# A fused attention, channel-mixing and expert kernel: the split channel weights are kept in DRAM and loaded as two parts

## The chip, the cores and the metric

The kernel runs on one core of a Trainium2 chip. Its engines each run their own instruction stream, in order: PE (matrix products, with PEld loading the stationary operand), DVE and ACT (element-wise work), POOL (element-wise work and indirect DMAs) and SP, which here issues all plain DMAs. An instruction that waits for a semaphore holds up everything behind it on its engine. The metric is device time in microseconds of one execution; a profile of one such execution gives the rows that are read below.

## The reference, cut to what matters

The program computes three blocks in a row for 4 batches of 576 tokens: attention in which scores more than `tau` below the row's maximum are dropped, a channel block, and a block of 8 experts of which each token takes one.

```
attn = softmax(where(scores >= max(scores) - tau, scores, -1e9)) @ v
u  = x + (x.T @ U @ V).T
y  = u + relu(u @ w_ch1) @ w_ch2          # 512 -> 2048 -> 512
e  = expert of the token (arg-max of logits, or the token before's)
out[b, s] = p[e] * (relu(y[b, s] @ w1[e]) @ w2[e])
```

All data are float32. The change is about `w_ch1` and `w_ch2`, the channel weights.

## The kernel before

**Split operands.** A product of the channel block is made of three faster ones: each operand is split into a high part of type F32R (ACT writes a copy of the float32 tile in that type) and a low part (the tile less its high part). The products are high by high, high by low and low by high, summed in PSUM. `w0h` and `w0l` are the parts of a chunk of `w_ch1`, `w1h` and `w1l` those of `w_ch2`; `uh`, `ul` those of the activations, `hh`, `hl` those of the hidden layer.

**Stages.** Attention of batch 0 runs first, alone. Then three mixed stages follow: the channel block of batch b-1 is interleaved with the attention of batch b (the costs 82 and 65 given to `interleave` set the mix). The channel block of batch 3 then runs beside the first steps of the experts (`early_slots`), and at last the experts run alone. The channel block goes over 16 chunks f of the hidden width: `mlp_l1(b, f)` (24 products, lines 610 to 612) for each chunk, and after the chunks 4, 8, 12 and at the end `mlp_l2` over four chunks (96 products, lines 627 to 629).

**How a chunk comes in.** The weights arrive as 64-bit floats. `convert` turns them into float32 once, in 512-column pieces (`cr` loads on line 180, ACT and DVE steps, stores to the DRAM tensor `wdram` on line 219), during the attention of batch 0 and the first mixed stage. `load_w(b, f)` (line 583) then serves every batch: for each of the two halves it loads a float32 tile `wr` of 256 KB from `wdram` (line 592), lets ACT write the high part (line 595) and POOL the low part (line 596). It is called two chunks ahead, at the end of chunk f for chunk f+2. `wr` has 6 buffers, `w0h`/`w0l` have 2 each and `w1h`/`w1l` 5 each. With 2 buffers the parts of chunk f+2 can be written only when `mlp_l1` of chunk f has read its own; with 5 buffers the `w1` parts of chunks 5 to 8 wait for the first `mlp_l2`, and so on.

**What sets the order.** The program is written in one order, and a scheduler with its own costs places each engine's instructions; only during the attention of batch 0 is POOL, and in the experts SP, held to the written order. SP's list thus mixes the weight loads with the attention's loads (`raw`, `v`), the conversion's loads and stores, the stores of finished rows (`ydram`, line 677) and the expert weights (`ew`, line 959).

**The experts' start.** The rows of the first expert are fetched by POOL with indirect DMAs into `yg` tiles (line 1023), which take buffers of the tag `wr`; PE turns them (`y0p`, `y1p`, `y2p`, line 1032), each into the same PSUM tile after ACT and DVE have emptied it (lines 1034, 1035).

Of the kernel before, what the change touches and what calls it, by code (L numbers as in the profile page):

```python
# [8 lines left out]
F32 = mybir.dt.float32  # L9
# [5 lines left out]
AF = mybir.ActivationFunctionType  # L15
ALU = mybir.AluOpType
# [6 lines left out]
FF = 2048  # L23
# [32 lines left out]
WR = 6  # L56
# [27 lines left out]
def attention_channel_moe(ctx, tc, qk, vv, tau, umat, vrep, wch, wgl, wexp, consts, out):  # L84
    nc = tc.nc
    pe, dve, act, pool, sp = nc.tensor, nc.vector, nc.scalar, nc.gpsimd, nc.sync

    cp = ctx.enter_context(tc.tile_pool(name="cp", bufs=1))
    dr = ctx.enter_context(tc.tile_pool(name="dr", bufs=1, space=DRAM))
    ydram = dr.tile([NTOK, DM], F32, name="ydram")  # L90
    wdram = dr.tile([FF, 1024], F32, name="wdram")

    cst = cp.tile([128, C_W], F32, name="cst")
    ident = cst[:, C_ID:C_ID + 128]
# [19 lines left out]
    mlp = p1.enter_context(tc.tile_pool(name="mlp", bufs=1))  # L114
# [468 lines left out]
    def load_w(b, f):  # L583
        nm = f"{b}_{f}"
        if f >= NF or nm in W:
            return
        while DONE[0] < f:
            next(conv, None)
        r = []
        for i, bufs in ((0, W0), (1, W1)):  # L590
            x = mlp.tile([128, 512], F32, tag="wr", name=f"wr{nm}_{i}", bufs=WR)
            sp.dma_start(out=x, in_=wdram[f * 128:f * 128 + 128, i * 512:i * 512 + 512])
            hi = mlp.tile([128, 512], F32R, tag=f"w{i}h", name=f"w{i}h{nm}", bufs=bufs)
            lo = mlp.tile([128, 512], F32R, tag=f"w{i}l", name=f"w{i}l{nm}", bufs=bufs)
            act.activation(hi, x, AF.Copy)  # L595
            pool.tensor_tensor(out=lo, in0=x, in1=hi.bitcast(F32), op=ALU.subtract)  # L596
            r.append((hi, lo))
        W[nm] = r

# [33 lines left out]
    def channel(b):  # L633
        hs = {}
        load_w(b, 0)
        load_w(b, 1)
        for f in range(NF):
            yield from mlp_l1(b, f, hs)
            if f % 4 == 0 and f:
                yield from mlp_l2(b, f - 4, hs)  # L640
            load_w(b, f + 2)
        HS[b] = hs
# [373 lines left out]
    rows, yts = {}, {}  # L1016
# [228 lines left out]
```

## Time and profile before

| | us |
|---|---|
| median of 3 runs | 1111.4 (1111.2 to 1113.02) |
| the profiled execution | 1110.32 |
| its span in the profile | 1108.5 |
| PE busy in the span | 1037.1 (94%) |
| attention alone / mixed stages / last channel block / experts (ends read from PE's rows) | 123 / 123 to 686 / 686 to 812 / 812 to the end |

The span is the profiled execution less what lies around it (1.8 us). A row of a table of stretches gives each engine's busy time in the stretch with its number of instructions, the granted clock of TensorE as a share of full speed, the mean busy share of the 16 DMA engines, and GB/s. Idle time of PE is what a change to its feeders can give back; idle time of another engine matters only where PE waits for it.

### The profile page before, as it was taken

The numbers are of one execution on the slowest core, as the hardware profiler recorded it, in microseconds if no ns is written. First come the engines' busy times: TensorE is split into PE (matmuls) and PEld (weight loads), VectorE is DVE, ScalarE is ACT, GpSimd is POOL, SyncE is SP. The second block draws the span as 40 slices with busy tenths as digits, with TensorE's granted clock in tenths as the row PEclk, the third lists the DMA queues.
The fourth block names the chain that finished last, engine by engine and source line by source line (L and its number), as shares of the span: only waits on it lengthen the run. The fifth ranks groups of instructions, "written<-read, shape, count | busy, mean of one in ns | idle before, by whom it ended". The sixth has DMA issues, their size and how long they took to land. (4 is left out here: it accounts for less than half of the span.)

```text
span 1108.5 us, 19450 instructions
## 1 busy us (share of the span) xinstructions
PE 1037.1 (94%) x7170; PEld 910.7 (82%) x7170; DVE 687.5 (62%) x1617; ACT 581.6 (52%) x1220; POOL 313.4 (28%) x246
## 2 busy tenths in 40 slices
PE   6788899999999999999999999999999999999995
PEld 4566788889888889988898998979878788889874
DVE  6898776776465666646656554552458664456573
ACT  5788676674554556546464554332333344445462
POOL 1221123142222314221241222234411433233231
PEclk9899999999999999999999999989999999999998
DMA  6544577762223124132321211352243465456550
GB/s 199 184 152 138 181 247 227 240 214 93 88 92 95 58 78 126 53 99 77 94 70 42 67 49 55 114 213 82 77 138 133 129 222 162 153 175 200 186 170 15
DMA packets 57992, 143.83 MB, mean 130 GB/s; under 512 B 7133, under 2 KB 7901, under 8 KB 57888
## 3 DMA queue, kind: packets, MB, share of 16 engines
q1 hardware_dynamic: 54528, 132.27, 37.4%
q0 software_dynamic: 3360, 10.23, 2.8%
q8 instruction: 58, 0.95, 0.4%
q14 instruction: 46, 0.38, 0.1%
HBM read 124.65 MB, written 18.61 MB: 129 GB/s over the span
## 5 line engine op out<-in xcount | busy, mean ns | idle before, releaser
L610 PE MATMUL l<-uh,w0h 128*128 128x256 f32 (+1 forms) x512 | 157.9, 308 | 4.5 <-DVE hl L614 2.1
L596 POOL TENSOR_TENSOR w1l<-wr,w1h 128x512 fp32r<-128x512 f32 x64 | 81.7, 1299 | 269.7 <-ACT w1h L595 246.2
L627 PE MATMUL l<-hh,w1h 128*128 128x256 f32 (+1 forms) x512 | 157.4, 307 | 0.2 <-DVE yT L630 0.2
L612 PE MATMUL l<-uh,w0l 128*128 128x256 f32 (+1 forms) x512 | 153.7, 300 | 2.8 <-POOL w0l L596 2.8
L596 POOL TENSOR_TENSOR w0l<-wr,w0h 128x512 fp32r<-128x512 f32 x64 | 85.0, 1327 | 243.4 <-ACT w0h L595 233.8
L611 PE MATMUL l<-ul,w0h 128*128 128x256 f32 (+1 forms) x512 | 153.3, 299 | 0.0
L628 PE MATMUL l<-hl,w1h 128*128 128x256 f32 (+1 forms) x512 | 152.8, 298 | 0.0
L629 PE MATMUL l<-hh,w1l 128*128 128x256 f32 (+1 forms) x512 | 152.2, 297 | 0.0
L1000 ACT ACTIVATE eh<-ew 128x512 fp32r<-128x512 f32 x160 | 94.4, 627 | 88.6 <-PE el L1116 46.4
L335 ACT ACTIVATE p<-s,st 128x576 f32<-128x576 f32 x144 | 104.5, 741 | 61.3 <-DVE st L324 61.1
L1002 DVE TENSOR_TENSOR el<-ew,eh 128x512 fp32r<-128x512 f32 x120 | 98.4, 840 | 41.9 <-ACT eh L1000 40.6
L339 DVE SCALAR_TENSOR_TENSOR p<-s,st,p 128x576 f32<-128x576 f32 x144 | 114.6, 815 | 15.2 <-ACT p L335 10.0
L324 DVE TENSOR_REDUCE st<-s 128x1 f32<-128x576 f32 x144 | 105.6, 751 | 28.4 <-PE s L291 26.4
L289 PE MATMUL s<-kh,qs 128*128 128x288 f32 x320 | 99.7, 330 | 17.8 <-DVE p L339 8.4
L388 ACT ACTIVATE ptt<-tp 128x512 f32<-128x512 f32 (+1 forms) x192 | 90.3, 494 | 41.5 <-PE tp L387 41.1
L614 DVE SCALAR_TENSOR_TENSOR hl<-l,hh 128x256 fp32r<-128x256 f32 (+1 forms) x128 | 58.1, 454 | 81.3 <-ACT hh L613 80.6
L630 DVE TENSOR_TENSOR yT<-l,yT 128x256 f32<-128x256 f32 (+1 forms) x128 | 58.2, 455 | 77.9 <-PE l L629 77.4
L610 PEld LDWEIGHTS l<-uh,w0h 128*128 128x128 f32 x512 | 97.4, 190 | 8.3 <-DVE hl L614 3.4
L612 PEld LDWEIGHTS l<-uh,w0l 128*128 128x128 f32 x512 | 97.4, 190 | 4.1 <-POOL w0l L596 3.0
L627 PEld LDWEIGHTS l<-hh,w1h 128*128 128x128 f32 x512 | 97.0, 190 | 3.9 <-issue 2.6
L387 PE MATMUL tp<-cst,p 128*128 128x128 f32 x576 | 94.5, 280 | 5.0 <-ACT ptt L388 4.8
L1002 POOL TENSOR_TENSOR el<-ew,eh 128x512 fp32r<-128x512 f32 x40 | 55.3, 1383 | 153.0 <-ACT eh L1000 133.2
(467 smaller groups left out, 2526.7 us busy)
## 6 DMA issues: line engine op xcount, KB each, us to landing
ew<-in_wexp_dram SPq DMA_DIRECT2D x80, 512.0 KB, 4.3
wr<-wdram SPq DMA_DIRECT2D x128, 256.0 KB, 2.9
cr<-in_wch_dram SPq DMA_DIRECT2D x32, 512.0 KB, 5.0
raw<-in_qk_dram SPq DMA_DIRECT2D x30, 304.0 KB, 3.1
wdram<-w SPq DMA_DIRECT2D x32, 256.0 KB, 2.7
v<-in_vv_dram SPq DMA_DIRECT2D x16, 352.0 KB, 3.1
raw<-in_qk_dram SPq DMA_DIRECT2D x16, 320.0 KB, 3.6
raw<-in_qk_dram SPq DMA_DIRECT2D x17, 288.0 KB, 3.0
```

The lines of the kernel that those rows point to most:

```text
L289: pe.matmul(s["t"][:, h, :288], lhsT=qs[:, qc:qc + 128], rhs=kh[:, k0:k0 + 288], start=(j == 0), stop=False)
L324: dve.tensor_reduce(out=self.st[:, 0, h:h + 1], in_=self.t[h], axis=AX.XY, op=ALU.max, negate=True)
L335: act.activation(self.halves(h), self.t[h], AF.Exp, bias=self.st[:, 0, h:h + 1])
L339: dve.scalar_tensor_tensor(out=p, in0=self.t[h], scalar=self.st[:, 1, h:h + 1], in1=p, op0=ALU.is_ge, op1=ALU.mult, accum_out=self.rvs[:, ...
L596: pool.tensor_tensor(out=lo, in0=x, in1=hi.bitcast(F32), op=ALU.subtract)
L610: pe.matmul(pm, lhsT=w1h[:, wk], rhs=uh[:, k, o:o + n], start=(k == 0), stop=False)
L611: pe.matmul(pm, lhsT=w1h[:, wk], rhs=ul[:, k, o:o + n], start=False, stop=False)
L612: pe.matmul(pm, lhsT=w1l[:, wk], rhs=uh[:, k, o:o + n], start=False, stop=(k == 3))
L627: pe.matmul(pm, lhsT=w2h[:, wd], rhs=hh[:, o:o + n], start=(f == f0), stop=False)
L628: pe.matmul(pm, lhsT=w2h[:, wd], rhs=hl[:, o:o + n], start=False, stop=False)
L629: pe.matmul(pm, lhsT=w2l[:, wd], rhs=hh[:, o:o + n], start=False, stop=(f == f0 + 3))
L1002: eng.tensor_tensor(out=lo, in0=x, in1=hi.bitcast(F32), op=ALU.subtract)
```

## The change

A second DRAM tensor, `wsplit`, holds for each row of weights the four parts side by side. In batch 0 `load_w` works as before and then stores the four parts there (four DMAs of 256 KB for each chunk). In the batches 1 to 3 it loads the four parts straight into their tiles: four DMAs of 256 KB in place of two, and neither ACT nor POOL takes part. In the changed kernel the lines stand lower: the load of `wr` is line 599, the stores are line 603, the direct loads line 606, `mlp_l1`'s products 620 to 622, the turning of `yg` 1042.

```
-            x = mlp.tile([128, 512], F32, tag="wr", name=f"wr{nm}_{i}", bufs=WR)
-            sp.dma_start(out=x, in_=wdram[f * 128:f * 128 + 128, i * 512:i * 512 + 512])
...
-            act.activation(hi, x, AF.Copy)
-            pool.tensor_tensor(out=lo, in0=x, in1=hi.bitcast(F32), op=ALU.subtract)
+            parts = [(y.bitcast(F32), wsplit[rows, c:c + 512]) for y, c in ((hi, i * 1024), (lo, i * 1024 + 512))]
+            if b == 0:
+                x = mlp.tile([128, 512], F32, tag="wr", name=f"wr{nm}_{i}", bufs=WR)
+                sp.dma_start(out=x, in_=wdram[rows, i * 512:i * 512 + 512])
+                act.activation(hi, x, AF.Copy)
+                pool.tensor_tensor(out=lo, in0=x, in1=hi.bitcast(F32), op=ALU.subtract)
+                for y, z in parts:
+                    sp.dma_start(out=z, in_=y)
+            else:
+                for y, z in parts:
+                    sp.dma_start(out=y, in_=z)
```

The order that the scheduler makes of it is shown at three places. The first is SP's list in the first mixed stage, where the chunks 6 and 7 of batch 0 are loaded (`wr0_7_0` is batch 0, chunk 7, half 0; `cr0_9_0` a load of the conversion for chunk 9). Before:

```order
L592 DMA wr0_6_1_2037<-wdram_61 128x512 [waits DMAHW6_49,DMAHW2_49]
L259 DMA raw7_0_2312<-in_qk_dram 128x576 [waits Pool_49]
L219 DMA wdram_61<-w0_7_0_1802 128x512 [waits DMAHW0_49,DVE_49]
L273 DMA v6_1747<-in_vv_dram 128x704 [waits DMAHW1_49,PE_49]
L180 DMA cr0_8_512_1853<-in_wch_dram 128x2048 [waits Activation_49]
L219 DMA wdram_61<-w0_7_512_1855 128x512 [waits DMAHW3_49,DVE_49]
L180 DMA cr0_9_0_1918<-in_wch_dram 128x2048 [waits DMAHW4_49,Activation_49]
L592 DMA wr0_7_0_2101<-wdram_61 128x512 [waits DMAHW5_49,DMAHW0_49]
L592 DMA wr0_7_1_2107<-wdram_61 128x512 [waits DMAHW6_49,DMAHW3_49]
```

Now, up to the same load:

```order
L603 DMA wsplit_62<-w0h0_6_2056 128x512 [waits DMAHW4_49,Activation_49]
L603 DMA wsplit_62<-w0l0_6_2057 128x512 [waits DMAHW5_49,Pool_49]
L221 DMA wdram_61<-w0_8_512_2001 128x512 [waits DMAHW6_49,DVE_49]
L603 DMA wsplit_62<-w1h0_5_1676 128x512 [waits DMAHW7_49,Activation_49]
L603 DMA wsplit_62<-w1l0_5_1677 128x512 [waits DMAHW0_49,Pool_49]
L603 DMA wsplit_62<-w1h0_6_2064 128x512 [waits DMAHW1_49,Activation_49]
L603 DMA wsplit_62<-w1l0_6_2065 128x512 [waits DMAHW2_49,Pool_49]
L182 DMA cr0_10_0_2089<-in_wch_dram 128x2048 [waits DMAHW3_49]
L599 DMA wr0_7_0_2132<-wdram_61 128x512 [waits DMAHW4_49]
```

Six stores, each waiting for ACT or POOL, now stand between the load of chunk 6 and that of chunk 7; the conversion has run one chunk further by then.

The second place is SP's list in the channel block of batch 3, where the expert weights `ew` come in between. Before, with loads that wait for POOL to have emptied a `wr` buffer:

```order
L959 DMA ew7_8229<-in_wexp_dram 128x1024 [waits DMAHW5_49]
L592 DMA wr3_10_0_9127<-wdram_61 128x512 [waits DMAHW6_49,Pool_49]
L592 DMA wr3_10_1_9133<-wdram_61 128x512 [waits DMAHW7_49,Pool_49]
L592 DMA wr3_11_0_9171<-wdram_61 128x512 [waits DMAHW0_49,Pool_49]
L592 DMA wr3_11_1_9177<-wdram_61 128x512 [waits DMAHW1_49,Pool_49]
```

Now, with loads that wait for PE to have read the chunk two before:

```order
L969 DMA ew4_8163<-in_wexp_dram 128x1024 [waits DMAHW6_49]
L606 DMA w0h3_7_8778<-wsplit_62 128x512 [waits DMAHW7_49,PE_49]
L606 DMA w0l3_7_8779<-wsplit_62 128x512 [waits DMAHW0_49,PE_49]
L969 ISA
L969 DMA ew5_8164<-in_wexp_dram 128x1024 [waits DMAHW1_49]
L606 DMA w0h3_8_8819<-wsplit_62 128x512 [waits DMAHW2_49,PE_49]
L606 DMA w0l3_8_8820<-wsplit_62 128x512 [waits DMAHW3_49,PE_49]
```

The loads are no longer issued ahead of need, and each pair of `w0` stands right behind 512 KB of expert weights.

The third place is PE's list where `mlp_l1` of chunk 7 of batch 3 begins. Before:

```order
L612 MATMUL l1_3_6_256_8898<-uh3_8061,w0l3_6_8827 128x320
L610 MATMUL l1_3_7_0_8928<-uh3_8061,w0h3_7_8871 128x256 [waits DVE_49]
L611 MATMUL l1_3_7_0_8928<-ul3_8062,w0h3_7_8871 128x256
L612 MATMUL l1_3_7_0_8928<-uh3_8061,w0l3_7_8872 128x256 [waits Pool_49]
L610 MATMUL l1_3_7_0_8928<-uh3_8061,w0h3_7_8871 128x256
```

Now:

```order
L622 MATMUL l1_3_6_256_8803<-uh3_7998,w0l3_6_8738 128x320
L1042 MATMUL y0p_9827<-cst_63,yg0_9813 128x128 [waits DMASW0_49]
L1042 MATMUL y0p_9827<-cst_63,yg0_9813 128x128 x3
L620 MATMUL l1_3_7_0_8829<-uh3_7998,w0h3_7_8778 128x256 [waits DMAHW7_49,DVE_49]
L621 MATMUL l1_3_7_0_8829<-ul3_7999,w0h3_7_8778 128x256
L620 MATMUL l1_3_7_256_8844<-uh3_7998,w0h3_7_8778 128x320 [waits DVE_49]
L621 MATMUL l1_3_7_256_8844<-ul3_7999,w0h3_7_8778 128x320
L622 MATMUL l1_3_7_0_8829<-uh3_7998,w0l3_7_8779 128x256 [waits DMAHW0_49]
```

The turning of the first gathered rows (`y0p`), which stood in and behind the last `mlp_l2` of the channel block, has moved ahead of chunk 7 and waits there for an indirect DMA; and two products that need only the high part stand ahead of the first that needs the low part.

## Rows read from the trace of the kernel before

**Rows 1.** The page: busy us of PE, its share of the span, instructions.

```profile
PE 1037.1 (94%) x7170; PEld 910.7 (82%) x7170; DVE 687.5 (62%) x1617; ACT 581.6 (52%) x1220; POOL 313.4 (28%) x246
```

**Rows 2.** Stretches, one per stage with a channel block; columns as told above.

```profile
123.00:303.00 180.00, 175.04 (x1316) 158.34 (x1316) 121.45 (x266) 114.96 (x243) 51.89 (x39) 1.00 0.59 187
303.00:496.00 193.00, 188.06 (x1427) 168.17 (x1426) 116.19 (x283) 106.80 (x231) 54.18 (x42) 1.00 0.27 84
496.00:686.00 190.00, 186.23 (x1412) 167.31 (x1415) 111.35 (x277) 100.87 (x221) 46.66 (x36) 1.00 0.20 64
686.00:812.00 126.00, 120.57 (x886) 113.80 (x887) 60.42 (x184) 38.52 (x81) 46.16 (x37) 0.97 0.34 115
```

**Rows 3.** PE's waits, 120 to 820 us: releaser, total us, times, longest.

```profile
PE s L289 <- DVE p L339: 3.4, 7, 1.1
PE l L612 <- POOL w0l L596: 2.8, 1, 2.8
...
PE lt L657 <- DVE yT L630: 0.2, 1, 0.2
```

**Rows 4.** Groups by line: busy us, mean ns; idle us before, releasers.

```profile
L595 ACT ACTIVATE w0h<-wr 128x512 fp32r<-128x512 f32 x64 | 40.5, 632 | 43.3 <-PE l L611 28.2 <-issue 11.6 <-POOL w1l L596 1.9
L595 ACT ACTIVATE w1h<-wr 128x512 fp32r<-128x512 f32 x64 | 37.4, 625 | 65.4 <-PE l L628 57.6 <-DMA wr<-wdram 7.8
...
L596 POOL TENSOR_TENSOR w0l<-wr,w0h 128x512 fp32r<-128x512 f32 x64 | 85.0, 1327 | 243.4 <-ACT w0h L595 233.8 <-PE l L612 4.4 <-DMA ydram<-yr 2.8
L596 POOL TENSOR_TENSOR w1l<-wr,w1h 128x512 fp32r<-128x512 f32 x64 | 81.7, 1299 | 269.7 <-ACT w1h L595 246.2 <-PE l L628 17.0 <-PE tb L440 3.6
```

**Rows 5.** PE in order of time, 792 to 796 us; in brackets the idle time before.

```profile
795.53 0.39 PE L612 MATMUL l<-uh,w0l 128*128 128x256 f32 x1 [2.75 <-POOL w0l L596]
```

**Rows 6.** POOL in order of time, 792 to 796 us.

```profile
793.00 1.27 POOL L1002 TENSOR_TENSOR el<-ew,eh 128x512 fp32r<-128x512 f32 x1
794.22 1.26 POOL L596 TENSOR_TENSOR w0l<-wr,w0h 128x512 fp32r<-128x512 f32 x1
```

**Rows 7.** PE in order of time, 819 to 822 us.

```profile
819.86 0.66 PE L1032 MATMUL y2p<-cst,yg 128*128 128x128 f32 x4 [1.61 <-DVE y0l L1035]
```

**Rows 8.** PE in order of time: chunks 6 and 7 of batch 3.

```profile
737.98 0.28 PE L610 MATMUL l<-uh,w0h 128*128 128x256 f32 x1
...
741.18 0.28 PE L610 MATMUL l<-uh,w0h 128*128 128x256 f32 x1
...
741.42 0.28 PE L612 MATMUL l<-uh,w0l 128*128 128x256 f32 x1
```

**Rows 9.** ACT in order of time: the buffer of chunk 5 of batch 3.

```profile
738.10 0.63 ACT L595 ACTIVATE w0h<-wr 128x512 fp32r<-128x512 f32 x1 [1.64 <-PE l L611]
```

**Rows 10.** The tile wr: SP's issue (ns min/median/max) and the landing.

```profile
L592 SPq DMA_DIRECT2D wr<-wdram x128: 319/320/1005, 40.3 to 768.9; - x128
...
DMA to landing us min/median/max: 2.5/2.9/6.1
```

**Rows 11.** ACT in order of time: two chunks of batch 1, mixed stage.

```profile
377.10 0.63 ACT L595 ACTIVATE w0h<-wr 128x512 fp32r<-128x512 f32 x1 [1.02 <-PE l L611]
...
381.80 0.63 ACT L595 ACTIVATE w0h<-wr 128x512 fp32r<-128x512 f32 x1
```

**Rows 12.** DVE in order of time: the indices of the first gathers.

```profile
737.11 0.17 DVE L882 CAST idxa<-iia 128x10 int32<-128x10 f32 x1
```

**Rows 13.** Line 1023, the gathers: from issue to landing.

```profile
DMA to landing us min/median/max: 3.3/3.6/5.8
```

**Rows 14.** Stretches of line 595 alone: ACT busy (count), clock, DMA share, GB/s.

```profile
130.00:250.00 120.00, 13.86 (x22) 1.00 0.75 235
```

**Rows 15.** Stretches in the first mixed stage, columns as in rows 2.

```profile
155.00:160.00 5.00, 4.61 (x30) 2.74 (x28) 3.71 (x8) 3.55 (x8) 0.36 (x1) 1.00 0.93 327
```

**Rows 16.** The tensor wdram: the conversion's stores, first and last start.

```profile
L219 SPq DMA_DIRECT2D wdram<-w x32: 319/326/606, 37.8 to 249.5; - x32
```

**Rows 17.** ACT's waits, 120 to 300 us.

```profile
ACT w1h L595 <- DMA wr<-wdram: 4.9, 3, 2.9
```

More of the change, by code (lines that the diff above doesn't have):

```diff
@@ L91, in attention_channel_moe @@
     wdram = dr.tile([FF, 1024], F32, name="wdram")
+    wsplit = dr.tile([FF, 2048], F32, name="wsplit")
     cst = cp.tile([128, C_W], F32, name="cst")
@@ L589, in load_w @@
         r = []
+        rows = slice(f * 128, f * 128 + 128)
         for i, bufs in ((0, W0), (1, W1)):
-            x = mlp.tile([128, 512], F32, tag="wr", name=f"wr{nm}_{i}", bufs=WR)
-            sp.dma_start(out=x, in_=wdram[f * 128:f * 128 + 128, i * 512:i * 512 + 512])
             hi = mlp.tile([128, 512], F32R, tag=f"w{i}h", name=f"w{i}h{nm}", bufs=bufs)
             lo = mlp.tile([128, 512], F32R, tag=f"w{i}l", name=f"w{i}l{nm}", bufs=bufs)
-            act.activation(hi, x, AF.Copy)
-            pool.tensor_tensor(out=lo, in0=x, in1=hi.bitcast(F32), op=ALU.subtract)
+            parts = [(y.bitcast(F32), wsplit[rows, c:c + 512]) for y, c in ((hi, i * 1024), (lo, i * 1024 + 512))]
[9 more added lines that the diff above has]
+                    sp.dma_start(out=y, in_=z)
             r.append((hi, lo))
```

## The prediction

> **What bounds the kernel now.** The page comes first. PE is busy for 1037.1 of 1108.5 us, ACT for 52% and POOL for 28% of the span [rows 1], so work that is taken from ACT and POOL shortens nothing by itself; only the time in which PE stands still for them can come back. The table by stage says where that can be [rows 2]: PE is idle for 4.96 of 180 us in the first mixed stage, 4.94 of 193 and 3.77 of 190 in the next two, and 5.43 of 126 in the last channel block (each the stretch less PE's busy time), 19.1 us in all. The list of PE's waits names what it stood for [rows 3]. It has fifteen lines between the first and the last shown, 21.7 us in sum, and one of them concerns the split weights: 2.8 us, once, for a low part from POOL. The other lines are softmax masks, copies of transposed tiles, row stores and routing. DMA is the third thing to read [rows 2]: its engines are busy 0.59 of the first mixed stage, but 0.20 to 0.34 of the later ones.
>
> **What the change removes.** In batches 1 to 3 it removes 3 x 16 x 2 = 96 steps of ACT of 0.63 us (60 us) and as many of POOL of 1.3 us (126 us) [rows 4]. Nearly all of it lies beside PE. Three things can come back.
>
> (a) The one wait: PE stood still for 2.75 us before the low part of the last chunk of batch 3 [rows 5], because POOL had first to do a split of expert weights (793.00) and only then this one (794.22) [rows 6]. The low part now comes by DMA. Gain 2.75 us, at worst 0 if the DMA is as late.
>
> (b) The gathers no longer wait for `wr` buffers that weights hold, so the scheduler moved the turning of the first gathered rows from the end of the channel block to the front of chunk 7. The chain of three turnings through one PSUM tile, which ends the block with 1.61 us of idle PE [rows 7], loses a link. I take 1.6, with 0 as the other end, since DVE and ACT are busy with routing there.
>
> (c) Fewer steps on ACT may shorten other waits. The list less the 2.8 us is 18.9 us. The 64 ACT steps of the two middle batches are 40 of 207.7 busy us of ACT in those stages [rows 2, 4], 19%; cut in that proportion the list would lose 3.6 us. The two lines nearest to PE in it, masks from DVE [rows 3], do not hang on ACT's load, so I take 0.5, between 0 and 3.6.
>
> **What it adds in the batches 1 to 3: loads just in time.** Before, `wr` was loaded ahead and the split took 0.63 + 1.3 = 1.96 us after PE had let go of the buffer. Now the DMA itself can start only then. In the last channel block the chunks follow at 3.20 us: `mlp_l1` starts at 737.98 and at 741.18 [rows 8], and the buffers of chunk 5 came free at 738.10, when ACT could write them [rows 9]. If SP issues the high part then and the low part 0.32 us later, and each lands 2.9 us after its issue [rows 10], they are there at 741.00 and 741.32. PE wants the high part at 741.18 and the low part at 741.42 [rows 8], and the order now puts two products (2 x 0.15 us) ahead of that. So it just fits at the median and is 3.0 us late at the longest landing, 6.1 us [rows 10]. Five chunks of batch 3 (7, 8, 11, 12, 15) come with no `mlp_l2` in between and at this pace. They share the queue with expert weights and follow bursts of `w1` parts. Bounds 0 and 5 x 3.0 = 15 us; the median is the nearer row, so I take 0.2 each, (d) 1.0. In the mixed stages the chunks follow at 4.70 us (377.10 to 381.80) [rows 11], which leaves 1.4 us to spare over 2.9 + 0.32; there I take nothing. SP waits for PE with the attention's loads behind it, but those run a pair of heads ahead, and PE's score products, which use them, come after those of the pair before.
>
> The Trainium skill (DMA: Bandwidth & Descriptors, Anatomy of one DMA) gives about 2.0 us plus the bytes at 436 GB/s for one DMA, measured on POOL's path; as an estimate from that page 256 KB take 2.6 us. By it both parts would land 0.3 us earlier, and (d) would be 0. The rows have 2.9 on SP's queue, and they decide.
>
> (e) The moved turning waits on PE for a gather. The indices were ready at 737.11 + 0.17 = 737.28 [rows 12]; the gather lands 3.6 us after its issue, at most 5.8 [rows 13], so at 740.9 to 743.1, and PE would reach it at 741.18. Between 0 and 1.9 us; nearest the median, 0.3.
>
> **What it adds in batch 0: stores.** 64 stores of 256 KB, 16.8 MB, most of them where DMA is fullest. Of the 32 splits of batch 0, 22 fall between 130 and 250 us [rows 14]; with two stores each that is 11.5 MB in 120 us, or 96 GB/s on top of 235, so 331 GB/s. What the engines can move is bounded from two rows: 235 GB/s at a share of 0.75 would be 313 at full [rows 14]; 327 GB/s at 0.93 would be 352 [rows 15]. By the second it fits; by the first the excess is (331 - 313)/313 x 120 = 6.9 us. Even then most of it is hidden: the conversion issues its last store at 249.5 [rows 16], and the stage that uses it goes on to 303. What is not hidden is the early part, where ACT already waits for `wr`, 4.9 us in three waits, the longest 2.9 [rows 17]; ACT's next steps, softmax ones, stand behind such a wait. SP's order adds to it: six stores now stand ahead of the load for chunk 7, each waiting for ACT or POOL. Four of them belong to splits that follow the end of an `mlp_l2`, 2 x (0.63 + 1.3) = 3.9 us [rows 4]; the chunk is needed two `mlp_l1` later, and at 4.7 us for one [rows 11] these cover it. Between 0 and 6.9 us; I take (f) 2.0, less than half of the 4.9 us again, since PE was idle for only 4.96 us in this stage even with those waits.
>
> **The sum.** -2.75 - 1.6 - 0.5 + 1.0 + 0.3 + 2.0 = -1.55 us. The profiled execution took 1110.32 us, so 1108.8; the median of the runs is 1.1 us higher, so 1109.9, or 1110. The measurement can tell about 0.2%, 2.2 us, from no change: below 1109.2 is faster, above 1113.6 slower.
>
> **Rivals.** First, the added transfers cost nothing: (d), (e) and (f) are 0, and -4.85 us remain, 1106.5. For it speak the later stages' DMA shares, 0.20 to 0.34 [rows 2], and the 352 GB/s [rows 15]; against it the 4.9 us of waits [rows 17].
>
> The Trainium skill (DMA: Bandwidth & Descriptors, Specifications) puts the limit of HBM for a core at about 358 GB/s. By it the 331 GB/s fit, (f) is 0, and this rival holds; no run here has shown more than 327 in five microseconds [rows 15].
>
> Second, the slower side: in the first mixed stage the stores fill the DMA engines, the conversion and the `wr` loads come late, and ACT stands still with the softmax behind it. It decides as soon as the engines move less than the 331 GB/s, and costs the 6.9 us in place of 2.0: 1110 + 4.9 = 1115. For it speaks the 0.75 share over 120 us [rows 14], against it that the conversion has time.
>
> Third, SP becomes the bound in the middle batches. A `w0` load stands behind a row store or an attention load that waits for ACT, DVE or POOL; once that holds SP longer than the 1.4 us to spare, PE stops. Eight chunks of a batch come without `mlp_l2` in between (2, 3, 4, 7, 8, 11, 12, 15). With 0.4 us each in two batches it is 6.4 us, 1116. Against it: ACT waited for PE in the same way before, in the same order, and PE did not stop.
>
> **How the numbers follow.** The forecast has a chance of 0.50 and a range of its own from 1107.5 to 1113; some 0.18 of it lies below 1109.2, 0.32 above. The first rival has 0.20 (faster), the second 0.15 (slower 0.13, same 0.02), the third 0.12 (slower), and 0.03 is left for a slower order that I don't see. Faster 0.38, same 0.34, slower 0.28. The range goes from 1105, below the first rival by a part of (c), to 1117, just above the third.
>
> **What would show it.** Right: no wait of PE for line 596 in the last channel block, PE waiting for loads of line 606 by a few tenths at chunks 7 to 15 of batch 3, a share of DMA of 0.9 or more from 130 to 250 us with PE's idle time there up by some 2 us, and middle stages of 193 and 190 us as before. Wrong: longer middle stages with PE waiting for line 606 (third rival), a first mixed stage longer by 5 us or more (second), or five microseconds gained in stages where I see nothing to gain.

## The result and the profile after

The changed kernel took 1121.0 us (median of 12 runs, 1117.0 to 1125.5), the kernel before 1112.8 us beside it (12 runs). The ratio is 1.0059, with a 95% interval from 1.0043 to 1.0075: slower by 0.6%. The forecast was 1110, the range 1105 to 1117; both missed on the slow side. The medians are over all runs, the ratio over the undisturbed ones.

The profiled execution took 1121.27 us and its span is 1119.4, 10.9 us more than before. The page of the changed kernel, first the busy times (us, share, instructions) that answer to [rows 1]:

```profile
PE 1043.7 (93%) x7170; PEld 914.8 (82%) x7170; DVE 669.2 (60%) x1617; ACT 532.6 (48%) x1124; POOL 187.3 (17%) x150
```

ACT and POOL have 96 steps less each, as the diff says, which is 49 us of work on ACT (the prediction had 60) and 126 on POOL. The span gained nothing by it. The table by stage, cut where the changed kernel's own stages end (columns as in [rows 2]):

```profile
123.00:312.90 189.90, 179.69 (x1324) 160.69 (x1323) 121.75 (x265) 112.02 (x236) 46.41 (x35) 0.99 0.76 249
312.90:503.60 190.70, 187.25 (x1421) 167.79 (x1417) 112.29 (x283) 89.89 (x197) 11.81 (x8) 1.00 0.41 129
503.60:693.30 189.70, 187.09 (x1417) 167.66 (x1417) 109.03 (x278) 85.35 (x189) 5.89 (x4) 1.00 0.35 108
693.30:826.10 132.80, 122.28 (x897) 114.42 (x893) 55.03 (x187) 26.45 (x59) 9.72 (x9) 0.99 0.54 177
```

The reader is to see that the first and the last stage grew (before: 180.7 and 127.0 us) and the middle two shrank (192.0 and 190.8). PE's idle time is the stretch less its busy time: 10.2 us in the first, 10.5 in the last. So a finer ruler is worth making. ACT copies each chunk's `mlp_l1` out of PSUM (line 623, before 613), and the start of the second half's copy is a time mark for that chunk; the end of DVE's last sum (line 640, before 630) marks the end of a channel block. Both exist in each kernel here, so two traces can be laid over each other. Lateness of the changed kernel against the one before, in us (a table worked out from the two traces):

```
mark               before   after   late    between marks
batch 0, chunk 4    149.7   152.5   +2.8
batch 0, chunk 8    199.6   205.1   +5.6
batch 0, block end  303.7   312.9   +9.3    batch 0            +9.3
batch 1, block end  495.7   503.6   +7.8    batch 1            -1.5
batch 2, block end  686.5   693.3   +6.8    batch 2            -1.0
batch 3, chunk 4    709.0   716.3   +7.3                       +0.5
batch 3, chunk 5    738.6   741.4   +2.8    chunk 4 to 5       -4.5
batch 3, chunk 7    745.0   751.0   +6.0
batch 3, chunk 8    748.2   756.4   +8.1
batch 3, chunk 11   770.6   784.1  +13.5    chunk 5 to 11     +10.7
batch 3, block end  813.5   826.1  +12.6    to the block's end -0.9
end                1108.5  1119.4  +10.9    tail               -1.7
```

Two places lose, 9.3 us in batch 0 and 10.7 between chunks 5 and 11 of batch 3, and the rest gains 9.1. PE's waits from 120 to 830 us, the answer to [rows 3] (releaser, total us, times, longest):

```profile
PE tp L389 <- ACT ptt L390: 6.0, 10, 1.5
PE l L620 <- DMA w0h<-wsplit: 3.5, 3, 1.4
PE l L622 <- DMA w0l<-wsplit: 3.2, 3, 2.4
PE y0p L1042 <- DMA yg<-ydram,idxa: 2.4, 1, 2.4
...
PE l L622 <- POOL w0l L601: 1.6, 2, 0.8
...
PE l L620 <- ACT w0h L600: 0.9, 1, 0.9
```

The 2.8 us for a low part from POOL [rows 3, 5] is gone, and so is the wait of 1.6 us for the chain of turnings [rows 7]. In their place stand 6.7 us for `w0` loads, all in batch 3, and 2.4 for the gather. A third kind grew, waits for ACT's copies of turned softmax tiles (`ptt`): 8.6 us on three lines, of which the first is shown, against 4.5 before; in batch 0 alone 5.3 against 2.9.

PE in order of time in the last block (start, us, instruction, in brackets the idle time before it):

```profile
746.96 0.65 PE L1042 MATMUL y0p<-cst,yg 128*128 128x128 f32 x4 [2.39 <-DMA yg<-ydram,idxa]
752.32 0.39 PE L620 MATMUL l<-uh,w0h 128*128 128x256 f32 x1 [1.35 <-DMA w0h<-wsplit]
753.39 0.38 PE L622 MATMUL l<-uh,w0l 128*128 128x256 f32 x1 [0.27 <-DMA w0l<-wsplit]
...
776.49 0.35 PE L620 MATMUL l<-uh,w0h 128*128 128x256 f32 x1 [0.97 <-DMA w0h<-wsplit]
779.51 0.58 PE L622 MATMUL l<-uh,w0l 128*128 128x256 f32 x1 [2.40 <-DMA w0l<-wsplit]
```

These are the steps at chunks 7, 8 and 11 of the ruler. The loads behind the last two waits are seen on SP's queue, in order of issue:

```profile
767.68 0.32 SPq L606 DMA_DIRECT2D w1h<-wsplit  x1
768.10 0.38 SPq L606 DMA_DIRECT2D w1l<-wsplit  x1
...
772.20 0.32 SPq L606 DMA_DIRECT2D w0h<-wsplit  x1
772.61 1.34 SPq L606 DMA_DIRECT2D w0l<-wsplit  x1
```

Six loads of 256 KB went out from 767.68 to 769.99. The `w0` loads, issued at 772.20 when their buffer came free, landed behind them. PE wanted the low part 4.5 us after its issue (779.51 less the 2.40 waited, less 772.61), and it landed 6.9 us after it. Of the four such pairs issued between 741 and 757 us the trace tells the landing of one, that of chunk 8, issued at 744.45 and 745.16 beside expert weights and gathers (min/median/max from issue to landing):

```profile
DMA to landing us min/median/max: 7.8/8.0/8.2
```

The DMA engines were nearly full then (columns as in [rows 2]):

```profile
744.00:753.00 9.00, 5.26 (x36) 4.42 (x35) 2.10 (x4) 1.85 (x4) 2.59 (x3) 1.00 0.95 350
```

Before, a `wr` load took 2.9 us at the median and 6.1 at most [rows 10], and PE never waited for one.

### The profile page after: what moved, and what is told of

It reads as the page before. It is cut to its first block, busy times and chain, and to the rows that moved or that the text cites. A ratio compares the mean times of both kernels' runs of the same rounds, so it can differ in the third digit from the quotient of the medians.

```text
span 1119.4 us, 19447 instructions
## 1 busy us (share of the span) xinstructions
PE 1043.7 (93%) x7170; PEld 914.8 (82%) x7170; DVE 669.2 (60%) x1617; ACT 532.6 (48%) x1124; POOL 187.3 (17%) x150
## 5 line engine op out<-in xcount | busy, mean ns | idle before, releaser
L620 PE MATMUL l<-uh,w0h 128*128 128x320 f32 (+1 forms) x512 | 158.9, 311 | 5.3 <-DMA w0h<-wsplit 3.5
L621 PE MATMUL l<-ul,w0h 128*128 128x320 f32 (+1 forms) x512 | 153.6, 300 | 0.0
L1012 DVE TENSOR_TENSOR el<-ew,eh 128x512 fp32r<-128x512 f32 x120 | 92.6, 789 | 44.6 <-ACT eh L1010 40.9
L291 PE MATMUL s<-kh,qs 128*128 128x288 f32 x320 | 101.1, 334 | 16.1 <-DVE p L341 6.5
L623 ACT ACTIVATE hh<-l 128x256 fp32r<-128x256 f32 (+1 forms) x128 | 52.1, 407 | 118.5 <-PE l L622 118.1
L621 PEld LDWEIGHTS l<-ul,w0h 128*128 128x128 f32 x512 | 98.2, 192 | 0.3
```

Of the source, the lines that this page charges most:

```text
L291: pe.matmul(s["t"][:, h, :288], lhsT=qs[:, qc:qc + 128], rhs=kh[:, k0:k0 + 288], start=(j == 0), stop=False)
L620: pe.matmul(pm, lhsT=w1h[:, wk], rhs=uh[:, k, o:o + n], start=(k == 0), stop=False)
L621: pe.matmul(pm, lhsT=w1h[:, wk], rhs=ul[:, k, o:o + n], start=False, stop=False)
L1012: eng.tensor_tensor(out=lo, in0=x, in1=hi.bitcast(F32), op=ALU.subtract)
```

## The experiments

Twelve kernels ran, each beside the kernel before. Two theories were held for batch 0: A, the stores' traffic fills the DMA engines; B, a store at the head of SP's queue waits for its split and holds back the loads behind it. For batch 3: `w0` loads that start only when a buffer comes free.

**Stores alone.**

```
-            if b == 0:
+            if True:
...
-                for y, z in parts:
+                for y, z in parts if b == 0 else ():
```

> Batch 0 stores its parts as in the changed kernel; batches 1 to 3 load the unsplit weights and split them on ACT and POOL as before. In the profile of the changed kernel the last result of batch 0's channel block is 9.4 us later than before (323.1 against 313.7), and 3 of these come back early in batch 1. Theory A (the stores' transfers fill the DMA engines of the first mixed stage): batch 0 again ends 8 to 11 us late, and the whole takes 1117 to 1123 us. Rival (the lateness of batch 0 is chance of one profile, or belongs to the loads that it prepares for batch 1): under 3 us late, 1110 to 1115 us.

Ratio 1.013 (1.0094 to 1.0165), 1129.1 us, above the range expected. Batch 0 ended 14.2 us late, and none of it came back in batches 1 and 2 (+14.3, +14.3). The last block kept its wait for POOL (2.7 us). So the stores cost as much and more without the loads, and the loads of parts are what gives back time later.

**Stores that wait for nothing.** The edit is against the kernel with the stores alone.

```
-                    sp.dma_start(out=z, in_=y)
+                    sp.dma_start(out=z, in_=cst[:, 0:512])
```

> As the kernel with the stores alone, but each store writes 512 columns of the resident constants, so that it waits for no split; wsplit, which nothing reads here, holds no weights. Same bytes, same queue. Theory A (traffic): batch 0 ends as late as with the real stores, 7 to 11 us, 1117 to 1123 us. Theory B (a store at the head of SP's queue waits for ACT or POOL to end the split, 16 + 12 + 7 + 7 us of such waits between 123 and 310 us in the changed kernel, and holds back the loads behind it): batch 0 at most 3 us late, 1111 to 1115 us.

Ratio 1.0062 (1.0038 to 1.0086), 1119.7 us. Batch 0 ended 6.4 us late, less than half of the 14.2 with real stores: neither theory alone. Stores that wait for nothing also go out earlier, before chunk 0 already (+3.7 us there), so this isn't a pure measure of traffic.

**Loads alone.**

```
-            parts = [(y.bitcast(F32), wsplit[rows, c:c + 512]) for y, c in ((hi, i * 1024), (lo, i * 1024 + 512))]
+            parts = [(y.bitcast(F32), wdram[rows, c:c + 512]) for y, c in ((hi, i * 512), (lo, 512 - i * 512))]
...
-                for y, z in parts:
-                    sp.dma_start(out=z, in_=y)
```

> No stores; batches 1 to 3 take both parts straight from wdram (each part is half of the unsplit row, so the weights of these batches are not the reference's), with the same number and size of loads as the changed kernel. Theory A (the just-in-time loads of w0 cost the last channel block about 10 us: +2.6, +2.2 and +5.3 us at its chunks 7, 8 and 11 in the changed kernel): these three steps come again, batch 0 is as before, and the sum of the other three batches and the rest is that of the changed kernel, -1.5 -1.0 +5.8 -1.7 = +1.6 us: 1111 to 1115 us. Rival (the waits in the last block were an accident of one profile): under 4 us of waits there, 1102 to 1108 us.

The total (1130.2 us, ratio 1.015, 1.0118 to 1.0182) says nothing on the loads: with other weights in batches 1 to 3 the routing changes, and from the last block's end on this kernel took 316.4 us (1127.0 less 810.6) with 7230 matmuls in place of 7170. I had not thought of that when I put totals into the expectation. The ruler up to that point holds: batch 0 +0.1, last block's end -3.0. Chunks 7, 8 and 11 of batch 3 again step up, by 1.9, 2.3 and 1.8 us, less than in the changed kernel. So up to there the loads alone are a gain of 3 us in this profile, net of waits.

**Only `w1` in parts.**

```
-            if b == 0:
+            if b == 0 or i == 0:
...
-                for y, z in parts:
+                for y, z in parts if i else ():
```

> Only the second half of each weight row (w1, five buffers) is stored in parts and loaded in parts; w0 (two buffers) is loaded unsplit and split on ACT and POOL in all batches. Theory A (half the stores, cost in proportion; no just-in-time loads): batch 0 ends 4 to 5 us late, the last block has no steps at chunks 7, 8 and 11, and of its gains a half or more is left, 3 to 6 us: 1108 to 1113 us. If the stage has a ceiling (DMA share up to about 0.8 costs nothing), batch 0 is under 2 us late and the whole takes 1104 to 1108 us.

Ratio 0.9945 (0.9924 to 0.9967), 1107.8 us: faster than before. Batch 0 +4.8, no step at chunks 7, 8 and 11, and -7.7 us within batch 3 (from +3.3 to -4.4). The changed kernel's batch 3 is +5.8 (from +6.8 to +12.6). Putting `w0` among the loaded parts costs 13.5 us there, one profile against one.

**More buffers for `w0`.**

```
-            hi = mlp.tile([128, 512], F32R, tag=f"w{i}h", name=f"w{i}h{nm}", bufs=bufs)
-            lo = mlp.tile([128, 512], F32R, tag=f"w{i}l", name=f"w{i}l{nm}", bufs=bufs)
+            spare = b > 0 and i == 0 and f in ((2, 3, 4, 7, 8, 9, 12, 15) if b == B - 1 else (2, 3, 4, 7, 8, 9, 12, 13, 14))
+            hi, lo = [mlp.tile([128, 512], F32R, tag="wr" if spare else f"w{i}{t}", name=f"w{i}{t}{nm}",
+                               bufs=WR if spare else bufs) for t in "hl"]
```

> The changed kernel, but in batches 1 to 3 the w0 parts of chunks 2, 3, 4, 7, 8, 9 and on go into the six idle wr buffers (three more pairs), so that a w0 load no longer waits for the product of two chunks earlier. Stores as in the changed kernel. Theory A (a w0 load that starts when its buffer comes free is what stops TensorE in the last block, beside the expert and w1 loads): the steps at chunks 7, 8 and 11 of batch 3 (+2.6, +2.2, +5.3 us) go, and the whole takes 1108 to 1114 us. Rival (it is the traffic of that block, whenever a load starts): at most half of the steps goes, 1115 to 1120 us.

Ratio 1.0009 (0.9988 to 1.003), 1115.7 us. The total is in the rival's range (1115 to 1120), but the steps, on which the two theories differ, are gone; batch 3 went from +14.5 to +6.2, a gain of 8.3. PE from chunk 5 to chunk 11 of batch 3, columns as in [rows 2]:

```profile
748.00:780.00 32.00, 32.00 (x242) 32.00 (x241) 9.16 (x20) 4.92 (x13) 2.19 (x2) 1.00 0.72 250
```

PE doesn't stop once in 32 us, at a higher rate of traffic (250 GB/s) than in the changed kernel's 42.7 us from chunk 5 to 11 (216). In nine of them the DMA engines were full:

```profile
748.00:757.00 9.00, 9.00 (x70) 9.00 (x69) 2.75 (x6) 2.46 (x6) 0.00 (x0) 1.00 1.03 408
```

The loads were nearly as slow as in the changed kernel (from 740 to 800 us; the trace tells 13 of 33 landings):

```profile
DMA to landing us min/median/max: 3.5/6.2/7.6
```

So it is the moment of issue that matters here: traffic makes a load slow, but PE sees it only where the load could not start earlier. The rival (traffic whenever a load starts) falls. Batch 0, which has the same code as the changed kernel, was 16.1 us late in this profile: the spread of that stage is large.

**Stores in batch 1.**

```
-            if b == 0:
+            if b < 2:
...
-                for y, z in parts:
+                for y, z in parts if b == 1 else ():
```

> All four parts are stored in batch 1, which still splits on ACT and POOL; batches 2 and 3 load the parts. In batch 1 the conversion is over, and the DMA share was 0.27 before. Theory A (stores cost only where the DMA engines are nearly full): batch 0 ends within 1 us of before, batch 1 at most 3 us late; batch 3 loses its 6 us again: 1112 to 1117 us. Rival (a store costs by its waits in SP's queue, wherever it is): batch 1 ends 5 to 9 us late, 1118 to 1124 us.

Ratio 0.9994 (0.9972 to 1.0017), 1114.7 us. Batch 0 +0.3, batch 1 +1.4 with all 64 stores, its DMA share 0.52. Batch 3 lost 2.1, with the steps again. Waiting stores hold SP here too, for 92.7 us in that batch, but cost 1 us. So a store's wait has no price of its own; what stands behind it in the queue, and what else the stage moves, are left to make the difference.

**Only `w1`, stored in batch 1.**

```
-            if b == 0:
+            if b < 2 or i == 0:
...
-                for y, z in parts:
+                for y, z in parts if b == 1 and i else ():
```

> Only the w1 parts, stored in batch 1 and loaded in batches 2 and 3; w0 is split on ACT and POOL throughout. If both causes are understood: batch 0 as before, batch 1 at most 2 us late, batch 2 1 us and batch 3 7 to 8 us gained as in the kernel that stores w1 alone in batch 0: 1101 to 1107 us. If the 5 us lost in batch 0 there were not the stores': no better than that kernel, 1107 to 1110 us.

Ratio 0.9924 (0.9906 to 0.9941), 1106.1 us. Batch 0 +1.1, batch 1 to +3.1 (2.0 lost), batch 3 from +2.2 to -5.4, 7.6 gained. As expected.

**Stores on POOL's queue.**

```
-                    sp.dma_start(out=z, in_=y)
+                    pool.dma_start(out=z, in_=y)
```

> The changed kernel with the stores issued from POOL's queue, behind the subtraction that makes the low part, so that no store stands in SP's queue; same bytes in the same stage. Theory B (half of the 9.4 us of batch 0 is the waits of stores at the head of SP's queue; stores that waited for nothing cost 6.7 us): batch 0 ends 4 to 7 us late, 1115 to 1119 us. Theory A alone (traffic): 8 to 10 us late, 1119 to 1123 us. If issuing takes POOL long, more than 10 us late.

Ratio 1.0186 (1.0138 to 1.0234), 1139.9 us, batch 0 20.4 us late: the third outcome. Issuing kept POOL busy for 0.55 us a store (54 of them between 123 and 303 us, 29.7 us), and on SP another wait grew, `wr` loads for the conversion's own stores to land:

```profile
SPq L599 <- DMA wdram<-w: 51.3, 21, 5.2
```

It was 4.5 us in the changed kernel, but 31.8 before (line 592 there), so by itself it is no sign of a loss. This run took the stores out of SP's queue, but gave POOL the issuing, so it doesn't decide between A and B, and why the stage is 20 us late is open.

**Stores one chunk later.**

```
...
-                for y, z in parts:
-                    sp.dma_start(out=z, in_=y)
+                late += parts
...
         W[nm] = r
+        if LATE:
+            for y, z in LATE.pop():
+                sp.dma_start(out=z, in_=y)
+        if late:
+            LATE.append(late)
```

> The changed kernel, but in batch 0 the four stores of a chunk are issued one chunk later, behind the next chunk's loads, when the split that they wait for is mostly done. Same bytes, same queue, same stage. Theory B (the part of batch 0's loss above the 6.4 us of the stores that waited for nothing is stores waiting at the head of SP's queue): batch 0 ends 4 to 7 us late, and the waits of the stores for ACT and POOL between 123 and 303 us fall under half; 1114 to 1119 us. Theory A (traffic and the loads it displaces): still 8 to 16 us late, 1118 to 1126 us.

Ratio 0.9984 (0.9969 to 0.9999), 1113.7 us; batch 0 +3.6. The same 64 stores. This decides for most of the loss. SP's waits before a store, 123 to 303 us, first the changed kernel (the largest five lines; all lines of its line 603 sum to 52.3 us), then this one (the largest two; its line 613 sums to 11.4):

```profile
SPq L603 <- ACT w0h L600: 16.4, 9, 3.8
...
SPq L603 <- POOL w0l L601: 11.6, 12, 1.0
...
SPq L603 <- ACT hh L623: 7.2, 5, 3.6
...
SPq L603 <- POOL w1l L601: 6.7, 12, 1.0
SPq L603 <- ACT w1h L600: 6.5, 2, 3.6
```

```profile
SPq L613 <- ACT w1h L603: 3.9, 2, 3.6
...
SPq L613 <- POOL w1l L604: 3.3, 4, 1.0
```

And the same 120 us as in [rows 14], all instructions: the kernel before, the changed one, the one with late stores (columns as in [rows 2]):

```profile
130.00:250.00 120.00, 115.13 (x864) 103.31 (x863) 86.01 (x183) 82.63 (x171) 37.27 (x28) 1.00 0.75 235
```

```profile
130.00:250.00 120.00, 110.83 (x811) 99.30 (x810) 80.85 (x171) 76.03 (x156) 31.38 (x24) 0.99 0.88 289
```

```profile
130.00:250.00 120.00, 113.27 (x837) 100.53 (x836) 78.64 (x176) 78.41 (x162) 33.38 (x25) 0.99 0.92 301
```

With late stores the engines moved more (301 GB/s against 289) and PE lost less. A stage that moves more when the order is better was not at a ceiling. The 3.6 us that are left here, and the 5.1 of another profile with late stores below, may be traffic or spread: kernels without any store in batch 0 ended it 0.1 to 3.6 us late.

**Both remedies in batch 1: stores there, spare buffers from batch 2.** The edit is that of the stores in batch 1, and `spare` with `b > 1`.

> Both remedies together: all four parts stored in batch 1, batches 2 and 3 load them, and w0 has the three spare pairs of wr buffers there. If the two causes add up as the runs so far say: batch 0 as before, batch 1 about 1.4 us late, batch 2 1 us gained, batch 3 8.3 us gained as with the spare buffers, end 7 to 9 us under before: 1102 to 1107 us, level with the kernel that stores only w1 in batch 1. Rival (stores of four parts and the deeper loads get in each other's way): 1109 to 1115 us.

Ratio 0.9953 (0.993 to 0.9976), 1110.8 us, in the rival's range. Batch 3 gained 8.3 (from +7.8 to -0.5) as foreseen, but batch 0 was 3.6 late though it has no stores, and batch 1 lost 5.2, where the run with stores in batch 1 had lost 1.1. In batch 1 PE was idle for 8.4 us against 4.9 before, with longer waits for a softmax copy (`ptt`, 2.3 against 0.2) and for `hl` (2.6 against 1.1), and the clock was at 0.50 for 3.4 us. What of it the stores cause, and what the spread of such stages, is open.

**Both remedies, stores in batch 0, one chunk later.** The edits of late stores and of more buffers for `w0` together.

> The changed kernel with two edits: the stores of batch 0 one chunk later, and w0's parts in batches 1 to 3 also in the six wr buffers. If the losses are the two places found (the stores that hold up SP's queue in batch 0, 5.7 of 9.3 us; the w0 loads that start when a buffer comes free, in batch 3): batch 0 ends 2 to 5 us late, batch 3 gains 8 us, no step at chunks 7, 8 and 11, and the whole takes 1102 to 1108 us. If the late stores gained in batch 0 by chance (a spread of its lateness of 9 to 16 us has been seen with the same code): 1109 to 1118 us.

Ratio 0.9901 (0.9872 to 0.9929), 1102.5 us: the fastest of all. Batch 0 +5.1, batch 3 from +3.1 to -5.0. Its last block, columns as in [rows 2]:

```profile
689.60:808.50 118.90, 117.69 (x893) 112.32 (x889) 54.46 (x186) 25.89 (x58) 9.60 (x9) 1.00 0.57 184
```

118.9 us against 132.8 in the changed kernel and 127.0 before; PE is idle for 1.2. Between 735 and 770 us its loads took up to 8.1 us to land, and PE waited for none:

```profile
DMA to landing us min/median/max: 3.1/6.0/8.1
```

**`w1` alone, stores one chunk later.** The edit of late stores, with `late += parts if i else []`, and `if b == 0 or i == 0`.

> As the kernel that stores w1 alone in batch 0 (it ended batch 0 4.8 us late and took 1107.8 us), with each chunk's two stores issued one chunk later. If half of the loss there is waits at the head of SP's queue: batch 0 ends 1 to 3 us late, 1103 to 1106 us. If it is traffic: no change, 1106.5 to 1109 us.

Ratio 0.9947 (0.9926 to 0.9968), 1107.0 us; batch 0 +5.3, no better than with the stores at once (+4.8). I had expected 1 to 3, and the total is in the range of the traffic rival. The delay did little to SP's waits at the `w1` stores here: 27.7 us against 31.1, with one wait of 14.4 us for ACT's copy still there. The waits stayed and so did the loss, which fits B, but the run doesn't show what traffic alone costs.

**Batch 0 over all profiles**, one profile each:

```
no store in batch 0       +0.1  +0.3  +1.1  +3.6          (loads alone, three with stores in batch 1)
64 stores one chunk late  +3.6  +5.1                      (SP's waits for the stores 11.4, 12.7 us)
32 stores of w1           +4.8  +5.3                      (31.1, 27.7 us)
64 stores, no wait        +6.4                            (0)
64 stores as in the change +9.3  +14.2  +16.1             (52.3, 50.6, 51.4 us)
64 stores from POOL       +20.4
```

The change's own stores, 9.3 to 16.1, stand clear of the late ones. The first four groups touch or overlap, and the spread inside a group is up to 7 us. SP's wait is no exact measure: no wait at all went with 6.4 us of lateness, 11.4 us of it with 3.6, and before the change SP waited 61 us at the `wr` loads of this stage. That it is what stands behind SP's wait that decides fits the runs in which SP waits for stores, but no run isolates it; the 6.4 us without any wait are another loss.

## Why the prediction was wrong, point by point

**Term (f), the stores, +2.0: the step that failed first. Measured +9.3 (14.2 and 16.1 in two other profiles of the same code).** The sum argued by GB/s: 331 wanted, ceiling 313 or 352. That was not where the loss lay. The late stores moved 301 GB/s at a share of 0.92 and lost 3.6; the kernel with both remedies moved 306 at 0.94. By the latter this mix would move 326 at full, an estimate, and the GB/s argument would be worth (331 - 326)/326 x 120 = 1.8 us. The prediction did name SP's order ("six stores now stand ahead of the load for chunk 7, each waiting for ACT or POOL"), and dismissed it with 3.9 us of splits that two `mlp_l1` cover. It priced the split's own time, not the wait for the split to begin. In the changed kernel (SP, in order of time):

```profile
179.15 0.56 SPq L599 DMA_DIRECT2D wr<-wdram  x1
...
182.35 0.43 SPq L599 DMA_DIRECT2D wr<-wdram  x1
182.82 0.43 SPq L182 DMA_DIRECT2D cr<-in_wch_dram  x1
186.60 0.32 SPq L603 DMA_DIRECT2D wsplit<-w0h  x1
187.97 0.32 SPq L603 DMA_DIRECT2D wsplit<-w0l  x1
...
189.88 0.32 SPq L603 DMA_DIRECT2D wsplit<-w1l  x1
190.43 0.32 SPq L221 DMA_DIRECT2D wdram<-w  x1
190.80 0.45 SPq L182 DMA_DIRECT2D cr<-in_wch_dram  x1
191.30 0.93 SPq L599 DMA_DIRECT2D wr<-wdram  x2
```

SP stood for 3.4 us before the store of `w0h`, and ACT shows why:

```profile
185.94 0.63 ACT L600 ACTIVATE w0h<-wr 128x512 fp32r<-128x512 f32 x1 [1.82 <-DMA wr<-wdram]
```

Both loads belong to chunk 7, the 15th and 16th of the kernel, and the copy waited for the first of them, issued at 179.15. So the store makes the queue wait out the landing of its own chunk's load, and the next load starts only then; before, loads ran ahead through six `wr` buffers and their landings overlapped. With stores one chunk later, the next chunk's loads stand ahead of the store again. The `wr` load at 191.30 is the 17th of the kernel, chunk 8's `w0`; before, the 17th was issued here:

```profile
173.19 0.33 SPq L592 DMA_DIRECT2D wr<-wdram  x1
```

A load that ran 18 us earlier now comes at the last moment; ACT waits for it, and here PE for ACT:

```profile
197.05 0.63 ACT L600 ACTIVATE w0h<-wr 128x512 fp32r<-128x512 f32 x1 [1.21 <-DMA wr<-wdram]
```

```profile
197.73 0.39 PE L620 MATMUL l<-uh,w0h 128*128 128x256 f32 x1 [0.89 <-ACT w0h L600]
```

Such direct waits are one half of what PE lost by waiting in this stage: 2.5 us for `w0h` and `w0l`, none before. Nearly as much came from its waits for the softmax copies `ptt`, 5.3 us against 2.9. ACT waited 11.1 us for `wr` in nine waits, 6.3 in four before, and most of PE's waits follow one of these within some 6 us (ACT at 172.87, PE at 178.20; ACT at 185.94 and 187.85, PE at 192.38); the longest, 1.5 us at 153.48, does not. So ACT's softmax steps stand behind its waits for `wr`, as term (f) had said of the kernel before, but this half of the account is read from the order in time and not shown.

Of the 9.3 us, 5.2 are idle time of PE (10.2 against 5.0) and 4.0 are more busy time. Of these, 1.7 come from the clock, an estimate (half of 3.4): the granted clock fell to 0.50, the lower of its two levels (1.2 GHz), at 199.2 us for 3.4 us, after 15 us in which PE had been idle for 2.5. The other 2.3 us of busy time I can't attribute.

**Second rival** (1115, chance 0.15): right in its place, its sign and nearly its size (6.9 us in that stage), right in the end of its chain (`wr` late, ACT still, softmax behind it) and wrong in the start: what made `wr` late was in the main the order in SP's queue, not full engines.

**Term (d), loads just in time, +1.0: measured 6.7 us of waits in batch 3** (1.35 + 0.27 + 0.97 + 2.40, 1.2 at chunk 15, and 0.56 at chunk 3, where nothing was taken), and 1.7 more for the clock by the same estimate: it stood at 0.50 for 3.4 us from 779.5, where the longest of the waits ended. The mechanism was right; the size was that of the median landing, 2.9 us [rows 10], and the waits lie between it and the bound of 15. The rows behind that median were loads issued ahead, with the engines less full: a share of 0.34 in that block [rows 2], against 0.95 from 744 to 753 us here. The text itself said that these would "share the queue with expert weights and follow bursts of `w1` parts", and then took the median of loads that did not. The Trainium skill (DMA: Bandwidth & Descriptors, Anatomy of one DMA) would give 2.6 us as an estimate for 256 KB alone, from its fit on POOL's path; the trace here has 7.8 to 8.2 for the pair of chunk 8, beside other loads.

**Term (e), the gather, +0.3: measured 2.4**, above its bound of 1.9. It is the same mistake: the gather's landing, 3.6 us, was taken from the gathers of the kernel before [rows 13]. Here the first one was issued at 740.80, as the loads of chunk 7 went out, and PE's wait for it ended at 746.96.

**Terms (a) and (b), -2.75 and -1.6: right as to the waits.** Both are gone (2.8 and 1.6). What (b) was worth can't be read off: the tail after the channel block gained 1.7 here, but in the other profiles it lies anywhere from 2.0 gained to 6.3 lost (the loads alone left out). With the `wr` buffers used for `w0`, (b) comes back: there PE waits 1.3 us for the chain again.

**Term (c), -0.5: too small.** Batches 1 and 2 gained 1.5 and 1.0. A larger gain was not in the sum at all: 4.5 us between chunks 4 and 5 of batch 3, where routing stands. PE's stretch there, before and after (columns as in [rows 2]):

```profile
709.00:738.60 29.60, 27.11 (x175) 22.64 (x175) 23.65 (x106) 5.53 (x11) 7.80 (x6) 0.88 0.52 188
```

```profile
716.30:741.40 25.10, 24.04 (x175) 20.78 (x176) 19.73 (x106) 2.61 (x5) 1.89 (x2) 1.00 0.55 189
```

The same 175 matmuls. Before, PE was idle for 2.5 us and then had 6.8 us at a clock of 0.50 (728.9 to 735.7), which cost 3.4, an estimate; after, it was idle for 1.1 and kept its clock. It waited for DVE, whose routing steps (`rha`, lines 866 and 867) came late beside POOL's splits of `w1`:

```profile
725.88 3.98 POOL L596 TENSOR_TENSOR w1l<-wr,w1h 128x512 fp32r<-128x512 f32 x3 [2.19 <-ACT w1h L595]
```

```profile
725.89 1.28 DVE L866 TENSOR_TENSOR rha<-rha,cst 96x10 f32<-96x10 f32 x1
727.21 1.19 DVE L867 TENSOR_TENSOR rha<-rha,p_all 96x10 f32<-96x10 f32 x1
```

```profile
728.45 0.64 PE L869 MATMUL pia<-r1a,rha 96*10 96x128 f32 x4 [1.56 <-DVE rha L867]
```

The median of these steps is 0.17 and 0.16 us, and in the changed kernel none of them took more than 0.17. All eleven profiles in which at least `w1` comes in parts in batch 3 have that step at 24.8 to 25.1 us in place of 29.6; the two that keep all splits there take 30.6 and 32.4. DVE's 106 steps in it take 19.7 to 20.0 us in the eleven, and 23.7 to 24.1 in those two and before. So the gain belongs to the change, and POOL being free beside DVE is the way that the traces show for the wait; that the clock fell because of it is not shown. The prediction had looked at ACT alone.

**First rival** (no cost) is refuted by (d) and (f). **Third rival** (SP in the middle batches) too: those stages got shorter.

**The fault common to (d), (e) and (f).** Each added transfer was priced by its own duration. Each was costly through its place: which instruction it stands in front of, and whether it can be issued before it is needed. Twice the prediction named that and then took the price of the undisturbed case.

## What to carry to other kernels

A DMA that is issued early may be slow for free, and one that is issued when its buffer comes free shows PE its landing in the traffic of that moment (7.8 to 8.2 us here), not the median of loads issued ahead (2.9); count buffers before exchanging a short on-chip step for a load. On an in-order queue a store must stand where its data is ready, or a load behind it that is needed soon comes late: moving the stores by one chunk took 9 to 16 us of loss to 4 or 5, with the same bytes. When a saving on idle engines is undone, look at the places of the new instructions first; both remedies together turned 0.6% slower into 1.0% faster than before. And work taken from an idle engine is not always worthless: ask whose steps run beside it.

## What was not expected of the hardware

A load of 256 KB took 2.9 us at the median when issued ahead, and 7.8 to 8.2 us in the one pair measured while all transfers together moved 350 GB/s at a share of 0.95. The DMA engines moved 408 GB/s for 9 us with loads of parts and expert weights, more than the 327 that the prediction had as the most seen and than the limit that its first rival cites; with the mix of the first mixed stage they moved 306 over 120 us at 0.94. A DVE step of 0.16 us took 1.2 to 1.3 us beside a step of POOL.

In three places PE stood idle for 2.5 to 3.4 us within some 15 us, and 3.4 or 6.8 us at a granted clock of 0.50 followed, so where such a wait went, up to 3.4 us more came back, an estimate. It is no rule: from 741 to 756 us in the changed kernel PE was idle for 4.0 us, and the clock stayed at 1.00 behind it, to 779. And lateness of one stage with the same code varied from 9 to 16 us between profiles, so a term of a few us there can be trusted only over several of them.
